# Attention probabilities transposed in pairs as 32-bit words, and two keys to a partition in the gathered V

## The chip, the core and the metric

The kernel runs on one core of a Trainium2 chip. The metric is the device time of one execution in microseconds (us), lower is better. A core has a matrix engine (TensorE, in the profile PE, with its weight loads as PEld), VectorE (DVE), ScalarE (ACT), GpSimd (POOL), and SyncE (SP), which here only issues DMA transfers. Operands lie in SBUF, 128 partitions wide; matrix results go to eight PSUM banks, each of 2 KB a partition, and have to be copied out by DVE or ACT. Sixteen DMA engines move data between HBM and SBUF.

## What is computed

Block-sparse attention over 4 batches x 8 heads x 768 positions x 64 channels, in blocks of 32 positions (24 blocks), followed by a dense two-layer network over all 3072 tokens:

```python
scores = scale * np.matmul(q, k.transpose(0, 1, 3, 2))
mask = np.abs(blk_i - blk_j) <= 1
mask = mask | (blk_i == 0) | (blk_j == 0) | (blk_i == n_blocks - 1) | (blk_j == n_blocks - 1)
for qb in range(n_blocks):
    for kb in sampled_blocks[qb]:                      # three drawn blocks
        mask[qb*32:(qb+1)*32, kb*32:(kb+1)*32] = True
attn = softmax(np.where(mask, scores, -1e9))
x = (attn @ v)                                          # tokens x 512
h = x @ w_in                                            # 512 -> 2048
out = (h * sigmoid(beta * h)) @ w_out                   # 2048 -> 512
```

A query block in the middle sees eight key blocks: three drawn ones, three of its window, and the two global ones (first and last). The first and last query blocks see all 24. Inputs and output are float32, `sampled_blocks` are 64-bit integers.

## The kernel before, in words

**Work and its order.** All of the program is a list of tasks, each with an engine (or a choice of engines), a duration that its author gave it, dependences and a priority. `Plan.run` places them in time like a small simulator, with rules for PSUM banks and a DMA ring, and the program is written out in that order; each engine then runs its instructions in it. The durations in the plan steer the order only. Tasks of the two-layer network have late priorities, so they fill PE where attention leaves it free.

**Middle blocks.** They are worked in pairs: 11 pairs a batch, 44 in all, task names with the pair number n. For a pair, POOL copies the drawn key blocks out of the transposed K into `KG` (L566, addresses from registers), POOL or DVE copy the window and, the first time, the global blocks (L261). PE adds a mask row by a matmul with ones (L658; it hides drawn blocks that repeat, and window blocks that repeat a global one) and multiplies queries with keys (L668). DVE takes maxima (L679), ACT the exponentials with sums (L687), DVE the reciprocals (L693), POOL or DVE scale the probabilities `PP` in fp16 (L699). PE transposes them, eight transposes of 128 x 128 for a pair (L711), DVE copies the bank to `PT` (L715), PE multiplies with `VG` in 32 matmuls of 64 x 32 (L727), and ACT or DVE put the result into `xT` (L259, L261).

**V.** `VG` holds the gathered V rows of a pair: 128 keys on the partitions, two halves of 512 channels and two query blocks in the free dimension. V of a batch is first written in fp16 to a table `VT` in HBM (L535, L539), a row of 512 channels being 1 KB, and SP gathers blocks from it (L627): the window (192 KB for both query blocks), the global blocks, and six drawn blocks of 32 KB. For the first four pairs the drawn rows don't come by DMA: PE picks them with one-hot matrices (`sel`, L388, made on DVE from block numbers that PE spreads over the partitions, L379 and L381), six matmuls of 512 columns for each query block (L638), which ACT or DVE copy into `VG` (L259, L261). Later pairs of a batch copy the global rows from an earlier `VG` (`vres`).

**Global blocks.** First and last query block are worked in 16 units (`gs` to `gav`): scores against all keys (L759), softmax (L773 to L791), six transposes with keys taken in steps of six (L799), DVE's copy to `PTG` (L801), 48 matmuls a batch with V (L813).

**The two-layer network.** `h` (L868), tanh on ACT (L874), the product on DVE (L879), `y` (L896), scaling and store (L265, L914 to L917). Its weights are loaded and cast by POOL's DMA queue (L461, L467), as are K, Q and V of batches 1 to 3 (L491).

**Start.** K, Q and V of batch 0 come through SP (L433), DVE casts them (L442), PE transposes (L508), ACT and DVE copy out. The 66 needed block numbers come by one DMA of single words (L291), from which POOL makes offsets (L307, L309) and DVE the mask (L313 to L337). One fp32 transpose exists, for beta (L402).

Of the kernel before, what the change touches and what calls it, by code (L numbers as in the profile page):

```python
# [10 lines left out]
FP32 = mybir.dt.float32  # L11
# [171 lines left out]
def kernel(  # L183
# [11 lines left out]
    nc = tc.nc  # L195
# [26 lines left out]
    SR, SG0, SN, SG1 = 0, 3, 4, 7  # L222

    identity = sb("identity", [P, P])
    ones = sb("ones", [P, P])
    maskr = sb("maskr", [P, NB - 2, 5])
    mrow = sb("mrow", [1, (NB - 2) * 5])
# [16 lines left out]
    PTG = sb("PTG", [P, J, 4, P])  # L244
# [26 lines left out]
    sbl = sb("sbl", [1, NB, 3], I32)  # L271
# [15 lines left out]
    def emit_sbl():  # L287
        src = sampled_blocks.tensor
        import dataclasses
        h = dataclasses.replace(src, shape=[NB, 6], dtype=I32)  # L290
        nc.scalar.dma_start(out=sbl, in_=bass.AP(tensor=h, offset=0, ap=[[0, 1], [6, NB], [2, 3]]))  # L291
    t_sbl = add("sbl", "ACT", 0.5, emit_sbl, prio=-200, dma=0.3, hw=1)
# [5 lines left out]
    sm5 = sb("sm5", [1, NB - 2, 5], FP32)  # L298
# [6 lines left out]
    def emit_idx():  # L305
        V = nc.gpsimd
        V.tensor_copy(out=sf, in_=sbl[:, 1:NB - 1, :])  # L307
# [5 lines left out]
    def emit_mask0():  # L313
        V = nc.vector
        V.memset(sm5, 0.0)
        V.memset(sm5[:, 0:1, 3:4], 1.0)
        V.memset(sm5[:, NB - 3:NB - 2, 4:5], 1.0)
# [12 lines left out]
    def emit_mask2():  # L330
# [4 lines left out]
        V.tensor_copy(out=sm5[:, :, 0:3], in_=sd)  # L335
        V.tensor_scalar(out=mrow, in0=sm5[:, :, :].rearrange("o a b -> o (a b)"),
                        scalar1=NEG / D, scalar2=None, op0=ALU.mult)  # L337
    t_mrow = None
    for part, f in enumerate((emit_mask0, emit_mask1, emit_mask2)):
        t_mrow = add(f"mask.{part}", "DVE", 0.95, f, deps=[t_idx, t_iota, t_ident, t_mrow], prio=-66.5)  # L340
    NM = (NB - 2) * 5
# [9 lines left out]
    SC = NSEL * 2 * 3 * BLK  # L351
    SH = SC // 2
    sel16 = sb("sel16", [P, SC])
    sel45 = sb("sel45", [P, 2, SC])
    sel = [xT[:, j // 2, N_TOK - (2 - j % 2) * SC:N_TOK - (1 - j % 2) * SC] for j in range(4)] + [
        sel45[:, i, :] for i in range(2)]
    srow = sb("srow", [1, NSEL * 2 * 3])
    mrow32 = sb("mrow32", [1, BLK])
    c32 = sb("c32", [1, P])
    pji = sb("pji", [P, J], I32)  # L360
    pj = sb("pj", [P, J], FP32)
    mi32 = sb("mi32", [1, BLK], I32)

    def emit_selc():
        V = nc.gpsimd
        V.iota(pji, pattern=[[1, J]], base=0, channel_multiplier=J, allow_small_or_imprecise_dtypes=True)
        V.iota(mi32, pattern=[[1, BLK]], base=0, channel_multiplier=0, allow_small_or_imprecise_dtypes=True)
        V.tensor_copy(out=pj, in_=pji)
        V.tensor_copy(out=mrow32, in_=mi32)
        V.memset(c32, float(BLK))  # L370
    t_selc = add("selc", "POOL", 1.2, emit_selc, prio=-98.5)
    t_srow = add("srow", "POOL", 0.15, lambda: nc.gpsimd.tensor_copy(
        out=srow, in_=sf[:, 0:2 * NSEL, :].rearrange("o a r -> o (a r)")), deps=[t_idx], prio=-98)
# [581 lines left out]
```

## Time and profile before

| | |
|---|---|
| median of 3 runs | 315.34 us (314.88 to 317.26) |
| the profiled execution | 316.81 us, of which the span from first to last instruction is 315.0 |
| busy: PE, DVE, ACT, POOL | 291.3, 232.1, 212.4, 185.4 us |
| L711, transposes of pairs | 352 matmuls, 28.4 us busy, 225 ns each |
| L799, transposes of global units | 96 matmuls, 8.2 us busy, 222 ns each |
| L727, probabilities times V | 1408 matmuls, 31.5 us busy |
| L638, picks | 48 matmuls, 15.9 us busy |
| L627, gathers of V | 306 DMAs of SP, most of 32 KB |
| queue q1 (SP's) | 27088 packets, 25.32 MB |

The time of one matmul in the profile includes its way through the array; matmuls overlap, so 225 ns is not what one more costs. That is read from the distance of their starts, or from how long a group of them lasts. The profile also gives, for every idle stretch of an engine, what ended it, and the chain of work that ended last. The granted clock is the share of full speed that the throttle let TensorE have.

### The profile page before, as it was taken

The numbers are of one execution on the slowest core, as the hardware profiler recorded it, in microseconds if no ns is written. First come the engines' busy times: TensorE is split into PE (matmuls) and PEld (weight loads), VectorE is DVE, ScalarE is ACT, GpSimd is POOL, SyncE is SP. The second block draws the span as 40 slices with busy tenths as digits, with TensorE's granted clock in tenths as the row PEclk, the third lists the DMA queues.
The fourth block names the chain that finished last, engine by engine and source line by source line (L and its number), as shares of the span: only waits on it lengthen the run. The fifth ranks groups of instructions, "written<-read, shape, count | busy, mean of one in ns | idle before, by whom it ended". The sixth has DMA issues, their size and how long they took to land.

```text
span 315.0 us, 12633 instructions
## 1 busy us (share of the span) xinstructions
PE 291.3 (92%) x4569; PEld 179.8 (57%) x4569; DVE 232.1 (74%) x536; ACT 212.4 (67%) x625; POOL 185.4 (59%) x534
## 2 busy tenths in 40 slices
PE   0889869998989899999999999999999999999994
PEld 0645558756946676556556565545655555554671
DVE  2972785988899999999985478999679845670160
ACT  1753757875876989778785579857679835671361
POOL 3389985988388797599687354648836842200000
PEclk9999956999999999999999999999999999999999
DMA  7969999699976886345899752234233341100201
GB/s 248 354 138 209 218 212 194 125 202 248 204 152 133 250 151 137 109 129 100 151 171 242 175 152 77 67 115 109 83 90 90 84 138 49 35 1 33 100 2 67
DMA packets 41546, 43.70 MB, mean 139 GB/s; under 512 B 6152, under 2 KB 37000, under 8 KB 41484
## 3 DMA queue, kind: packets, MB, share of 16 engines
q1 hardware_dynamic: 27088, 25.32, 27.8%
q0 software_dynamic: 10784, 11.27, 24.1%
q10 hardware_dynamic: 3612, 6.30, 5.5%
q8 instruction: 36, 0.59, 0.8%
q14 instruction: 26, 0.21, 0.2%
HBM read 44.70 MB, written 9.44 MB: 172 GB/s over the span
## 4 chain that ended last, share of the span: by engine, by line
PE 68%; DMA 7%; DVE 7%; issue 5%; POOL 4%; SPq 3%; POOLq 1%; ACT 1%; DVEq 0%; ACTq 0%
PE bank L868 23%; PE bank L896 22%; PE bank L727 7%; PE bank L711 6%; DMA RQ<-in_q_dram 6%; PE bank L668 2%; SPq L627 2%; PE bank L658 2%; POOL KG L566 2%; PE bank L508 2%; DMA VG<-VT 1%; PE bank L638 1%; DVE SG L773 1%; POOLq L561 1%; DVE ST L679 1%
## 5 line engine op out<-in xcount | busy, mean ns | idle before, releaser
L699 POOL TENSOR_SCALAR PP<-PP,ST 128x256 f16<-128x256 f16 x176 | 83.5, 490 | 35.7 <-DVE ST L693 31.1
L868 PE MATMUL bank<-xT,w_in_sb 128*128 128x256 f16 (+1 forms) x512 | 94.9, 332 | 1.9 <-DVE g L879 1.3
L687 ACT ACTIVATE PP<-bank,ST 128x256 f16<-128x256 f32 x176 | 81.6, 485 | 17.5 <-DVE ST L679 14.3
L896 PE MATMUL bank<-w_out_sb,g 128*128 128x512 f16 x384 | 91.3, 380 | 0.8 <-DVE g L879 0.8
L874 ACT ACTIVATE t<-bank,beta_sb 128x512 f16<-128x512 f32 (+1 forms) x128 | 70.0, 595 | 18.6 <-PE bank L868 15.5
L879 DVE SCALAR_TENSOR_TENSOR g<-t,bank 128x512 f16<-128x512 f16 (+1 forms) x128 | 66.4, 547 | 19.6 <-ACT t L874 19.2
L566 POOL COPY KG<-KT 128x64 f32 x264 | 53.9, 253 | 34.1 <-PE bank L668 26.7
L868 PEld LDWEIGHTS <-w_in_sb 128*128 128x128 f16 x512 | 54.2, 115 | 26.5 <-issue 4.8
L679 DVE TENSOR_REDUCE ST<-bank 128x2 f32<-128x512 f32 x88 | 57.3, 680 | 10.7 <-PE bank L668 10.6
L896 PEld LDWEIGHTS <-g 128*128 128x128 f16 x384 | 34.7, 98 | 39.2 <-issue 4.5
L715 DVE COPY PT<-bank 128x1024 f16<-128x1024 f16 x44 | 30.2, 685 | 14.1 <-PE bank L711 13.6
L687 ACT ACTIVATION_READ_ACCUMULATOR PP<-bank,ST 128x1 f32 x176 | 38.2, 217 | 0.0
L727 PEld LDWEIGHTS <-VG 128*64 128x64 f16 x1408 | 27.4, 115 | 17.3 <-issue 13.1
L727 PE MATMUL bank<-PT,VG 128*64 128x32 f16 x1408 | 31.5, 186 | 4.3 <-issue 2.1
L265 ACT ACTIVATE osb<-bank 128x512 f32<-128x512 f32 x24 | 14.4, 599 | 22.8 <-PE bank L896 22.7
L711 PE MATMUL bank<-identity,PP 128*128 128x128 f16 x352 | 28.4, 225 | 0.5 <-DVE PTG L801 0.3
L711 PEld LDWEIGHTS <-PP 128*128 128x128 f16 x352 | 23.0, 100 | 7.6 <-POOL PP L699 0.9
L780 ACT ACTIVATE PG<-bank,SG 128x384 f16<-128x384 f32 x32 | 18.3, 578 | 5.2 <-DVE ST L693 2.3
L668 PE MATMUL bank<-KG,QT 64*32 64x256 f16 x704 | 18.8, 278 | 0.9 <-POOL KG L566 0.8
L791 POOL TENSOR_SCALAR PG<-PG,SG 128x768 f16<-128x768 f16 x14 | 13.2, 946 | 9.4 <-ACT PG L780 3.8
L259 ACT CAST xT<-bank 128x256 f16<-128x256 f32 x25 | 9.5, 381 | 12.8 <-PE bank L727 11.0
L773 DVE TENSOR_REDUCE SG<-bank 128x1 f32<-128x384 f32 x32 | 16.1, 546 | 0.6 <-PE bank L759 0.5
(94 smaller groups left out, 261.7 us busy)
## 6 DMA issues: line engine op xcount, KB each, us to landing
VG<-VT SPq DMA_DIRECT2D x244, 32.0 KB, 2.8
VG<-VT SPq DMA_DIRECT2D x40, 192.0 KB, 3.8
out_dram<-osb ACTq DMA_DIRECT2D x20, 256.0 KB, 2.2
RV<-in_v_dram POOLq DMA_DIRECT2D x6, 384.0 KB, 5.8
RK<-in_k_dram POOLq DMA_DIRECT2D x6, 384.0 KB, 6.3
RQ<-in_q_dram POOLq DMA_DIRECT2D x6, 384.0 KB, 6.0
VT<-Vn SPq DMA_DIRECT2D x3, 768.0 KB, 6.0
w_in_sb<-in_moe_w_in_dram POOLq DMA_DIRECT2D x8, 256.0 KB, 8.0
```

Of the source, the lines that this page charges most:

```text
L566: nc.gpsimd.tensor_copy(out=kg32[:, g, :, (SR + r) * W:(SR + r + 1) * W], in_=kt32[:, :, bass.ds(vals[3 * g + r], W)])
L668: nc.tensor.matmul(bk[u][hp * BLK:(hp + 1) * BLK, g * 256:(g + 1) * 256], lhsT=QT[b % 2][u * D:(u + 1) * D, hp, (i0 + g) * BLK:(i0 + g + 1 ...
L679: mx[n, u] = add(f"mx{n}.{u}", "DVE", 0.6, lambda n=n, u=u, sb_=sb_: nc.vector.tensor_reduce(out=sb_[:, 0, 2 * u:2 * u + 2], in_=bank(("S" ...
L687: nc.scalar.activation(out=pb[:, u, g, :], in_=bank(("S", n, u))[:, g * 256:(g + 1) * 256], func=AF.Exp, bias=sb_[:, 0, 2 * u + g:2 * u + ...
L699: (nc.vector if eng == "DVE" else nc.gpsimd).tensor_scalar(out=pb[:, u, g, :], in0=pb[:, u, g, :], scalar1=sb_[:, 2, 2 * u + g:2 * u + g + ...
L711: nc.tensor.transpose(out=o[:, s * P:(s + 1) * P], in_=pb[:, u, g, c * P:(c + 1) * P], identity=identity)
L715: ptv[n] = add(f"ptv{n}", "DVE", 0.61, lambda n=n: nc.vector.tensor_copy(out=PT[n % NPT], in_=bank16(("T", n))), deps=[tp[n]] + ([av[n - N ...
L727: nc.tensor.matmul(o[us, (g * NHP + hp) * BLK:(g * NHP + hp + 1) * BLK], lhsT=vgb[:, g, c, (2 * hp + u) * D:(2 * hp + u + 1) * D], rhs=pt[ ...
L868: nc.tensor.matmul(o[:, 0:TW], lhsT=w_in_v[:, c, f // 4, f % 4, :], rhs=xT[:, c, c0:c0 + TW], start=(c == 0), stop=(c == NHP - 1))
L874: lambda G=G, f=f, TW=TW, tt=tt: nc.scalar.activation(out=tt[:, 0:TW], in_=bank(("H", G, f))[:, 0:TW], func=AF.Tanh, bias=0.0, scale=beta_ ...
L879: lambda G=G, f=f, TW=TW, tt=tt, gg=gg: nc.vector.scalar_tensor_tensor(out=gg[:, f, 0:TW], in0=tt[:, 0:TW], scalar=1.0, in1=bank(("H", G, ...
L896: nc.tensor.matmul(o[:, :], lhsT=gg[:, f, s * P:(s + 1) * P], rhs=w_out_sb[:, f, :], start=(f == 0), stop=(f == N_FFC - 1))
```

## The change

- **Transposes.** Two neighbouring fp16 probabilities are read as one 32-bit word. A pair takes four fp32 transposes instead of eight fp16 ones, a global unit three instead of six. A partition of `PT` and `PTG` then holds two neighbouring keys, even and odd in turn, so the matmuls with V read every second element.
- **V in step with it.** A partition of `VG` holds two neighbouring V rows (2 KB that lie together in `VT`), a block 16 partitions instead of 32. Each gather moves the same bytes as 16 rows of 2 KB.
- **Picks by parity.** The one-hot matrices choose row pairs, three of them instead of six. For one pair, two groups (even and odd rows) of three matmuls each yield both query blocks at once; four copies of 48 rows take them to `VG` instead of two of 96 rows.
- **Order of key blocks.** Global blocks lie together at the end (slots 6 and 7) instead of at 3 and 7; the mask has four columns a block instead of five, and the mask matmul of the first and last pair of a batch writes four key blocks instead of five.
- **Block numbers.** They come with their upper halves in one contiguous row.
- **A full fp32 identity** is made on DVE (before, a corner of 4 x 4); the one-hot matrices get tiles of their own instead of a corner of `xT`.
- The plan's durations for some of these tasks and for the first three key copies are new.

```diff
-    sbl = sb("sbl", [1, NB, 3], I32)
+    sbl = sb("sbl", [1, NB, 6], I32)
...
-        nc.scalar.dma_start(out=sbl, in_=bass.AP(tensor=h, offset=0, ap=[[0, 1], [6, NB], [2, 3]]))
+        nc.scalar.dma_start(out=sbl, in_=bass.AP(tensor=h, offset=0, ap=[[0, 1], [6, NB], [1, 6]]))
...
     t_id32 = add("id32", "DVE", 0.2, lambda: nc.vector.tensor_copy(
-        out=ident32, in_=identity[0:4, 0:4]), deps=[t_ident], prio=-64)
+        out=ident32, in_=identity), deps=[t_ident], prio=-64)
...
     t_sel = [add(f"sel16.{j}", "DVE", 0.27, lambda j=j: nc.vector.tensor_scalar(
         out=sel[j], in0=sel16, scalar1=pj[:, j:j + 1], scalar2=None, op0=ALU.is_equal),
-        deps=t_selw, prio=-66.2) for j in range(J)]
+        deps=[t_selw], prio=-66.2) for j in range(JP)]
...
-        kg[n] = add(f"kg{n}", "POOL", 1.15, emit_kg, deps=[t_idx] + kdeps, prio=pr)
+        kg[n] = add(f"kg{n}", "POOL", (1.5, 2.6, 1.35)[n] if n < 3 else 1.15, emit_kg, deps=[t_idx] + kdeps, prio=pr)
...
                 for r in range(3):
                     yield 0.1, lambda v, g=g, r=r: (
-                        vgb[r * BLK:(r + 1) * BLK, g, 0, :], vt[bass.ds(v[3 * g + r], BLK), :])
+                        vgb[(SR + r) * HB:(SR + r + 1) * HB, g, :, :],
+                        vt[bass.ds(v[3 * g + r], BLK), :].rearrange("(x e) m -> x e m", e=2))
...
-        for g in range(2 if n < NSEL else 0):
-            def emit_pick(n=n, g=g):
-                for j in range(J):
-                    c = (2 * n + g) * 3 * BLK
-                    nc.tensor.matmul(bank(("V", n, g))[0:3 * BLK, :], lhsT=sel[j][:, c:c + 3 * BLK],
-                                     rhs=Vn[0][:, j, :], start=(j == 0), stop=(j == J - 1))
+        for e in range(2 if n < NSEL else 0):
+            def emit_pick(n=n, e=e):
+                c = n * P
+                for j in range(JP):
+                    nc.tensor.matmul(bank(("V", n, e))[:, :], lhsT=sel[j][:, c:c + P],
+                                     rhs=Vn[0][:, 2 * j + e, :], start=(j == 0), stop=(j == JP - 1))
...
+            for g in range(2):
+                picked.append(add(f"pickv{n}.{e}.{g}", {"DVE": 0.61, "ACT": 0.58}, None,
+                                  lambda eng, n=n, e=e, g=g, vgb=vgb: copy_on(
+                                      eng, vgb[0:3 * HB, g, e, :],
+                                      bank(("V", n, e))[4 * HB * g:4 * HB * g + 3 * HB, :]),
+                                  deps=[tk], prio=pr - PK, closes=(("V", n, e),)))
...
-            ns = 5 if p in (0, NPAIR - 1) else 3
+            ns = 4 if p in (0, NPAIR - 1) else 3
...
         def emit_tp(n=n, pb=pb):
-            o = bank16(("T", n))
+            o = bank(("T", n))
             for g in range(2):
-                for c in range(2):
-                    for u in range(2):
-                        s = (g * 2 + c) * 2 + u
-                        nc.tensor.transpose(out=o[:, s * P:(s + 1) * P],
-                                            in_=pb[:, u, g, c * P:(c + 1) * P], identity=identity)
-        tp[n] = add(f"tp{n}", "PE", 0.45, emit_tp, deps=[nrm[n]], prio=pr - 0.5, lat=0.2,
+                for u in range(2):
+                    w = g * 2 + u
+                    nc.tensor.transpose(out=o[:, w * P:(w + 1) * P],
+                                        in_=pb[:, u, g, :].bitcast(FP32), identity=ident32)
+        tp[n] = add(f"tp{n}", "PE", 0.36, emit_tp, deps=[nrm[n], t_id32], prio=pr - 0.5, lat=0.2,
...
-                                rhs=pt[:, g, c, u, hp * BLK:(hp + 1) * BLK],
+                                rhs=pt[:, g, u, hp * BLK:(hp + 1) * BLK, c],
...
             def emit_gt(m=m, pg=pg):
-                o = bank16(("GT", m))
-                pj = pg[:, :].rearrange("x (p j) -> x j p", j=J)
-                for j in range(J):
-                    nc.tensor.transpose(out=o[:, j * P:(j + 1) * P], in_=pj[:, j, :], identity=identity)
+                o = bank(("GT", m))
+                pw = pg[:, :].bitcast(FP32).rearrange("x (p j) -> x j p", j=JP)
+                for j in range(JP):
+                    nc.tensor.transpose(out=o[:, j * P:(j + 1) * P], in_=pw[:, j, :], identity=ident32)
...
-                            rhs=PTG[:, j, u::2, hp * BLK:(hp + 1) * BLK],
+                            rhs=PTG[:, j // 2, u::2, :].rearrange("x w (m e) -> x w m e", e=2)[:, :, hp * BLK:(hp + 1) * BLK, j % 2],
```

## The prediction

> **What bounds the kernel now.** I read the page's chain by engine first, then the stage table (busy time of each engine in five stretches that I chose), then the chain and the timeline of the stretches that the diff touches, and last the single groups.
>
> ```profile
> PE 68%; DMA 7%; DVE 7%; issue 5%; POOL 4%; SPq 3%; POOLq 1%; ACT 1%; DVEq 0%; ACTq 0%
> 13.00:35.00 22.00, 19.94 (x200) 10.94 (x194) 13.41 (x33) 11.42 (x34) 20.07 (x57) 1.00 0.92 196
> 35.00:48.00 13.00, 8.93 (x250) 7.13 (x243) 9.86 (x24) 8.72 (x35) 11.37 (x28) 0.65 1.07 220
> 48.00:110.00 62.00, 58.47 (x1090) 42.45 (x1090) 54.79 (x141) 48.12 (x152) 46.38 (x123) 0.96 0.87 188
> 110.00:275.00 165.00, 163.04 (x2786) 94.94 (x2781) 133.82 (x286) 122.02 (x368) 104.80 (x312) 1.00 0.48 117
> ```
>
> The columns of the last four are the stretch, its length, busy us of PE, weight loads, DVE, ACT and POOL, the granted clock, the DMA engines' share and GB/s. From 110 to 275 us PE is busy 163 of 165: time taken from PE there comes off the end. From 13 to 48 us POOL (31.4 of 35) and the DMA engines (0.92, then 1.07) are full, and PE is not. So every edit is priced by where it falls: PE time counts in full from 48 us on, and before it only where the chain runs over PE.
>
> **The transposes (L711, L799).** Removed: 352 + 96 transposes of 128 two-byte columns; added: 176 + 48 of 128 four-byte words. Everything hangs on what one word transpose costs.
>
> ```profile
> 212.96 0.49 PEld L711 LDWEIGHTS <-PP 128*128 128x128 f16 x8
> 213.02 0.61 PE L711 MATMUL bank<-identity,PP 128*128 128x128 f16 x8
> 16.05 0.55 PEld L402 LDWEIGHTS bank<-t,osb 4*128 4x128 f32 x4 [0.17 <-issue]
> 16.05 0.64 PE L402 MATMUL bank<-t,osb 4*128 4x4 f32 x4
> 14.63 1.49 PE L508 MATMUL bank<-identity,RQ 128*64 128x128 f16 x24 [1.07 <-ACT QT L265]
> 123.10 0.79 PE bank L508 x24
> 42.95 1.02 PE bank L711 x8
> ```
>
> Now: eight in 0.61 us of which the last lasts 0.219, so (0.61 - 0.22)/7 = 0.056 us each, 0.45 us a pair; six of L799 0.336. The nearest row for a word is L402, the beta transposes: 128 words loaded, 4 columns streamed. Four loads of 0.208 (mean) lie in 0.55 us, so they start (0.55 - 0.21)/3 = 0.113 apart; its matmuls (0.64, mean 0.262) give 0.126. I take 0.12. PE ran at about half speed then: L508's 24 transposes take 1.49 us at 14.63 and 0.79 at 123.10 (the clock column shows 1.00 before 25 us only because nothing was recorded). At full speed 0.12 becomes 0.06. What 124 more columns add is not in the trace, so I bound it:
> - 0.06, if the next load runs beside the stream, as L711's loads do: 4 in 0.24, 0.21 saved a pair and 0.156 for each of the 16 global units, 44 x 0.21 + 16 x 0.156 = 11.7 us saved.
> - 0.113, if load and stream take turns: 0.06 + 124 columns at 0.43 ns (0.056/128). A pair costs 0.45, as now.
> - 0.267, if a word needs four streams. At half speed a two-byte transpose of 128 columns takes (1.02 - 0.31)/7 = 0.10, so a load of 128 words should too; the rest of L402's 0.12, some 0.015, is more than the 0.003 of four single columns, and would be four times four. At full speed 0.05 for the load and 4 x 0.054 for the streams.
>
> I take 0.10: L402's spacing is more than its load alone, which speaks for taking turns, with a little overlap. Saved: 44 x (0.45 - 0.40) + 16 x (0.336 - 0.30) = 2.8 us.
> The Trainium skill ("TensorE: Matmul & The Clock Gate", Terms, the row on the xbus) says that trn2's transpose mode is four times faster for FP32; by that rule the four-stream end falls away, and the sum with it. Against the change stands the same page's section on weight-path perf modes: fast weight load is not used with FP32 input, so a word load is slow and harder to hide; L402's load (0.208, against 0.098 of L711, though at the lower clock) agrees, and a sum by this rule loses the 2.8 us of the transposes.
>
> **AV and the global AV (L727, L813).** They now read every second element of PT and PTG. The chain has 48 matmuls of 64 columns (L813) in 0.76 us at 79.21 and 32 of 32 columns (L727) in 0.49 at 79.97: 16 ns and 15 ns. Twice the columns cost nothing, so the 64-column loads set the pace and a stream of half speed is still covered in AV. Without that cover, 13 ns on 32 columns: up to 16 pairs of matmuls x 13 ns x 44 = 9 us. I take 0.
> DVE's copies of PT and PTG move the same elements from the same banks: 0. The mask matmuls (L658) lose 64 of 320 columns in 8 pairs of 44: 0.2 us in all.
>
> **The head: picks, selection, block numbers.** Picks (L638) go from 48 to 24 of 512 columns.
>
> ```profile
> 29.79 1.29 PE bank L638 x6
> 31.50 1.43 PE bank L638 x6
> 33.38 1.29 PE bank L638 x6
> 36.60 1.38 issue
> 35.03 0.58 PEld L727 LDWEIGHTS <-VG 128*64 128x64 f16 x32 [0.21 <-DMA VG<-VT]
> DMA to landing us min/median/max: 4.0/7.1/12.4
> ```
>
> They are 4.0 us of the chain just ahead of the first AV; half is 2.0. But that AV starts 0.21 us after it could, on a VG transfer: without the picks the transfer is next, and 0.2 is all that comes unless it lands sooner. The last line is L627's (the VG gathers) from 14 to 50 us: up to 12.4 us to land. All VG rows now go as 2 KB runs instead of 1 KB. Prices from the queue table: q10's 3612 packets (6.30 MB, 5.5% of 16 engines' 315 us) take 77 ns for a mean of 1.7 KB; q1's 27088 (25.32 MB, 27.8%) take 52 ns for a mean of 0.93 KB. So 2 KB costs about 90 ns against 2 x 56, a fifth less. From 21 to 110 us 6.4 MB of VG are gathered: 3200 x 22 ns / 16 engines = 4.4 us less of queue. SP issues as many DMAs as before, 16 rows for 32. I take 1.5 us at the first AVs (between 0.2 and 3.4, the 2.0 of picks plus the 1.38 of the AV that sat at 36.60) and 1 us from the K, Q and V loads of batch 1 (11.1 us of the chain wait for RQ at 67 to 78; bounds 0 and 4.4).
> Block numbers come as one run of 576 bytes instead of 72 single words; POOL waits for them till 6.06 us. Eight small DVE mask operations then lie at 6.3 to 8.1 and five at 9.0 to 10.1, ahead of the second pair of K casts at 10.00. Six selection compares of 0.40 (2.4 us) become three of about 0.3. That brings K's cast about 0.9 us forward, and POOL's key copies at 13.24, with which the chain goes on, wait for K (ACT's KT): 0.9 us. If K's own transfer is late, 0.
> Added: evictions of picks go from 8 to 16, of the same columns (0.58 on ACT, 0.69 on DVE): 4.9 us. ACT has 10.6 and DVE 8.6 us idle from 13 to 35, which hides them; without that cover the last, 0.6 us, is late for the first AV. The full word identity on DVE (128x128, about 0.25 by the cast of maskr) lies before 6 us. POOL gains one small memset (0.2) in its idle time up to 13.24.
>
> **Sum.** 2.8 + 0.2 + 1.5 + 1.0 + 0.9 = 6.4 us off. The profiled execution took 316.81 (span 315.0 and 1.8 around it), 1.5 above the median of the runs, 315.34. So about 310.4 for an execution like the profiled one, and 309.0 for the median.
>
> **Rivals.**
> 1. A word is dear because four bytes stream at half speed: twice 0.054 for the stream, once or twice that for the load, taking turns: 0.16 to 0.213 a transpose. For it: L402 streams only four columns, so no row shows a word stream at two-byte speed. Against it: its four columns add no more than 0.02 to the load. Place: PE, L711 and L799, in the stretch where PE is full; price 224 x 0.16 - 25.2 = 10.6 to 22.5 us more, less the other 3.6: 322 to 334. It decides from 224 x cost = 25.2 + 3.6, that is 0.129 us a word transpose.
> 2. Four streams, 0.267: 34.6 us more, less 3.6: 346. For it speaks L402's spacing, as worked out; against it that the spacing may hold a fixed gap instead. The Trainium skill ("FP8 and Floating Point Precision", TensorE Precision Notes) counts four passes for a true FP32 product; L402 cannot tell whether that holds for a transpose, and the rule of the four times faster mode speaks against it.
> 3. Loads run beside the streams, 0.06: 11.7 + 3.6 off, 300. Then POOL (105 of 165 us) and DVE (134) are still below PE, so most of it arrives: 300 to 305.
> 4. The head gives nothing and the word transpose costs as now. A new order from the planner, the longer wait for VG, or PE at half clock for longer (0.65 from 35 to 48 now, after idle PE; fewer picks leave it idler) takes the 3.6 back: 313 to 318. Here belongs that the gathers still move 1 KB at a time: then q1's packets don't fall.
>
> **Chances.** Forecast (305 to 312) 0.38; rival 3 0.17; rival 4 0.17; rival 1 0.17; rival 2 0.11. A measurement of this kernel tells about 1% (3.2 us) from no change. Faster: forecast and rival 3, 0.55; within 1%: 0.17; slower: rivals 1 and 2, 0.28. The range reaches from rival 3's lower end to rival 1's upper: 300 to 334, leaving out rival 2 and a little below. The likeliest case alone: 305 to 312.
>
> **What would show it.** L711's matmuls: four with starts 0.10 apart and about 0.4 us a pair in the chain; 0.06 or 0.16 and more are the rivals. L727's 32 still in 0.5 to 0.6 us. The first AV at about 32.5 instead of 35.0, the first L868 at about 45 instead of 47.8. q1 at some 19,500 packets with the same MB. The first KG copy of POOL at about 12.3. The prediction is wrong if the word transposes start more than 0.129 us apart, or if the first L868 comes no sooner.

## The result: slower by 7.6%, and the profile after

| | before | after |
|---|---|---|
| median (lowest to highest) of 4 executions | 316.29 us (314.88 to 317.26) | 343.68 us (338.29 to 347.0) |
| ratio, 95% interval | | 1.076 [1.062, 1.089] |
| the profiled execution, its span | 316.81, 315.0 us | 345.37, 343.3 us |

Ratios here and below leave out executions that were disturbed, medians don't; the profiles of the changed kernel, of its two versions with nothing repaired but the stores (words and fp16), and of the changed work in the order of before come from executions that were left out, so what is read there of SP's waits is given from another profile too. Lines have moved: L627 is now L631 (gathers of V), L711 L718 (pairs' transposes), L727 L734 (probabilities times V), L799 L806, L868 L875, L896 L903.

The chain by engine, the stage table over the same stretches (stretch, length, busy us of PE, weight loads, DVE, ACT and POOL, granted clock, DMA share, GB/s), SP's queue and two groups of the changed kernel:

```profile
PE 48%; DMA 20%; DVE 14%; SPq 6%; ACT 4%; issue 4%; POOL 2%; POOLq 1%; DVEq 0%; ACTq 0%
13.00:35.00 22.00, 12.75 (x164) 5.94 (x158) 17.03 (x35) 10.84 (x33) 19.73 (x60) 0.84 0.88 186
35.00:48.00 13.00, 6.45 (x165) 4.76 (x166) 4.55 (x14) 5.84 (x25) 5.71 (x19) 0.50 0.92 174
48.00:110.00 62.00, 57.64 (x990) 42.76 (x989) 53.84 (x135) 45.41 (x144) 42.38 (x107) 0.94 0.84 170
110.00:275.00 165.00, 146.37 (x2322) 85.76 (x2321) 124.23 (x264) 110.72 (x340) 100.19 (x303) 0.95 0.47 113
q1 hardware_dynamic: 18576, 25.32, 25.2%
L734 PE MATMUL bank<-PT,VG 128*64 128x32 f16 x1408 | 33.2, 189 | 22.7 <-DMA VG<-VT 15.6
L718 PE MATMUL bank<-ident,PP 128*128 128x128 f32 x176 | 30.3, 296 | 12.7 <-POOL KG L565 7.8
```

PE's share of the chain has fallen from 68 to 48%, and DMA's has risen from 7 to 20. From 110 to 275 us PE now idles 18.6 of 165 us; it idled 2.0 before. PE's work has not grown: it is busy 293.2 us, before 291.3. The products with V (L734) wait 15.6 us for gathered rows, but 10.5 of that lies between 30 and 60 us and only 1.3 between 110 and 275. There most of the idle time is two stretches, 5.9 us up to 158.5 and 7.8 us up to 238.1, and both come through DVE. When DVE's next instruction copies global rows that SP has gathered (`vres`), and these are late, everything behind it is late too: the first time pair 21's PT, the second time the softmax of the global units, for which POOL waits 7.7 us. DVE's waits for such rows (us in total, times, longest):

```profile
DVE VG L264 <- DMA VG<-VT: 14.2, 2, 8.0
```

Half the clock (0.50) is granted from 158 to 164 and from 233 to 243 us. Of all twenty profiles, DVE waits like this (4.3 to 15.6 us) in the eight where SP's gathers wait over 40 us for stores, and in none of the other twelve. So the loss is waiting, and the waiting is for V.

What SP, which issues those gathers, waited for (line, what ended the wait, us in total, times, longest). Before:

```profile
SPq L627 <- PE bank L727: 16.2, 8, 6.6
SPq L627 <- DMA VT<-Vn: 4.8, 2, 2.5
SPq L627 <- DMA out_dram<-osb: 0.9, 1, 0.9
```

After:

```profile
SPq L631 <- DMA out_dram<-osb: 56.0, 12, 10.0
SPq L631 <- DMA VT<-Vn: 14.7, 1, 14.7
SPq L631 <- PE bank L734: 1.9, 4, 1.0
```

Before, SP ran so far ahead that it waited for a VG tile to come free (L727, 16.2 us). Now it waits 56 us for **output stores**, 4.7 us each time on average, and it has nothing to do with them: ACT issues them. The link is in the waits of the program. The DMAs of SP and ACT report their end on eight semaphores in rotation, and a DMA may use one only when the DMA eight places earlier in the program's list has landed. The Trainium skill says why it must wait ("DMA: Bandwidth & Descriptors", Why a DMA increments its semaphore by 16 and not by 1): with two DMAs in flight on one semaphore the count can reach the first one's mark before that one has fully landed, so each wants one of its own. The same page (Anatomy of one DMA) has such a wait happen on the issuing sequencer; the trace agrees, as SP's own queue stands still.

One such case in the changed kernel, first SP's and ACT's timelines (start, length, line, operation), then the chain (start, length, what):

```profile
130.77 8.23 SPq L631 DMA_DIRECT2D VG<-VT  x4
135.98 0.34 ACTq L923 DMA_DIRECT2D out_dram<-osb  x1
```

```profile
151.01 0.72 SPq L594
151.85 0.33 SPq L631
152.23 4.67 DMA VG<-VT
157.00 0.70 DVE VG L264
157.72 0.70 DVE PT L722
158.47 1.04 PE bank L734 x32
```

SP issues four gathers in 8.23 us, because one of them waits 6.4 us for the store that ACT can issue only at 135.98, when `y` and its scaling are done; the store lands at 138.17 and the gather, on the same semaphore, goes at 138.19. After that SP needs 0.5 us for a DMA, seven for a pair, and doesn't catch up: the global rows of the third batch's first pair are issued at 151.85, land at 156.9, DVE copies them at 157.0 and only then pair 21's PT, and PE's product with V follows at 158.47. PE is busy 17.81 of the 25 us from 150 to 175. In the second stretch the chain itself runs over a store, SP and the copy:

```profile
225.65 2.00 DMA out_dram<-osb
227.67 0.33 SPq L631
...
232.51 2.10 DMA VG<-VT
234.70 1.30 DVE VG L264 x2
```

The second loss is at the head. Timelines of SP and POOL in the changed kernel:

```profile
14.55 2.06 SPq L534 DMA_DIRECT2D VT<-Vn  x2
31.34 2.70 SPq L631 DMA_DIRECT2D VG<-VT  x6
```

```profile
15.26 1.98 POOL L460 DMA_DIRECT2D w_in_sb<-in_moe_w_in_dram  x3 [0.30 <-POOL w_in_sb L446]
```

POOL's key copies start at 10.42 instead of 13.24, and so the weights' loads, which stand behind them on POOL, at 15.26 instead of 19.66. V's table is stored only 1.9 us sooner, at 14.55 instead of 16.48. So the first weight load now starts before the table's second half (15.26 against 16.08) and two more right behind it, by 16.72, and the second half lands at 31.3; the first gather waits 14.7 us for it. Before, it landed at 21.5, with the weights' loads behind it. The first product with V starts at 38.6 instead of 35.0, the first with `w_in` at 53.4 instead of 47.8, and PE idles half of the time from 35 to 48 us, with half the clock granted (0.50). This second loss is not in every execution of this order: see the fp16 version below. The Trainium skill ("TensorE: Matmul & The Clock Gate", Part 1: The HAM clock gate) gives half clock after an idle window of about 3.4 us; the trace agrees as far as it goes: PE is busy 1.42 us from 24 to 28, and 0.50 is granted from 28 us on.

### The profile page after: what moved, and what is told of

Its sections match the earlier page's. It is cut to its first block, busy times and chain, and to the rows that moved or that the text cites. A ratio compares the mean times of both kernels' runs of the same rounds, so it can differ in the third digit from the quotient of the medians.

```text
span 343.3 us, 12204 instructions
## 1 busy us (share of the span) xinstructions
PE 293.2 (85%) x4319; PEld 179.6 (52%) x4319; DVE 237.2 (69%) x536; ACT 211.9 (62%) x627; POOL 183.7 (54%) x537
## 3 DMA queue, kind: packets, MB, share of 16 engines
q1 hardware_dynamic: 18576, 25.32, 25.2%
## 4 chain that ended last, share of the span: by engine, by line
PE 48%; DMA 20%; DVE 14%; SPq 6%; ACT 4%; issue 4%; POOL 2%; POOLq 1%; DVEq 0%; ACTq 0%
PE bank L875 17%; PE bank L903 16%; DMA VG<-VT 12%; PE bank L734 5%; SPq L631 5%; DMA VT<-Vn 4%; PE bank L718 4%; ACT PP L694 2%; DVE ST L686 2%; DMA out_dram<-osb 2%; DVE g L886 2%; PE bank L507 2%; DVE PT L722 1%; PE bank L675 1%; DMA g<-in_k_dram 1%
## 5 line engine op out<-in xcount | busy, mean ns | idle before, releaser
L706 POOL TENSOR_SCALAR PP<-PP,ST 128x256 f16<-128x256 f16 x172 | 81.3, 488 | 62.7 <-DVE ST L700 59.9
L875 PE MATMUL bank<-xT,w_in_sb 128*128 128x256 f16 (+1 forms) x512 | 96.3, 335 | 0.3 <-DVE g L886 0.3
L903 PE MATMUL bank<-w_out_sb,g 128*128 128x512 f16 x384 | 92.6, 383 | 0.6 <-ACT PP L694 0.4
L875 PEld LDWEIGHTS <-w_in_sb 128*128 128x128 f16 x512 | 55.6, 115 | 26.6 <-issue 5.3
L903 PEld LDWEIGHTS <-g 128*128 128x128 f16 x384 | 35.5, 98 | 39.9 <-issue 5.1
L734 PE MATMUL bank<-PT,VG 128*64 128x32 f16 x1408 | 33.2, 189 | 22.7 <-DMA VG<-VT 15.6
L734 PEld LDWEIGHTS <-VG 128*64 128x64 f16 x1408 | 29.2, 119 | 38.1 <-issue 26.5
L718 PE MATMUL bank<-ident,PP 128*128 128x128 f32 x176 | 30.3, 296 | 12.7 <-POOL KG L565 7.8
L694 ACT ACTIVATION_READ_ACCUMULATOR PP<-bank,ST 128x1 f32 x176 | 37.4, 212 | 0.0
L718 PEld LDWEIGHTS bank<-ident,PP 128*128 128x128 f32 x176 | 21.6, 148 | 20.6 <-POOL KG L565 8.4
L262 ACT CAST xT<-bank 128x256 f16<-128x256 f32 x30 | 11.2, 374 | 32.5 <-PE bank L734 19.2
L787 ACT ACTIVATE PG<-bank,SG 128x384 f16<-128x384 f32 x32 | 18.3, 592 | 14.7 <-DVE SG L782 11.7
L780 DVE TENSOR_REDUCE SG<-bank 128x1 f32<-128x384 f32 x32 | 16.1, 545 | 2.0 <-PE bank L766 2.0
```

The source lines that it names most:

```text
L694: nc.scalar.activation(out=pb[:, u, g, :], in_=bank(("S", n, u))[:, g * 256:(g + 1) * 256], func=AF.Exp, bias=sb_[:, 0, 2 * u + g:2 * u + ...
L706: (nc.vector if eng == "DVE" else nc.gpsimd).tensor_scalar(out=pb[:, u, g, :], in0=pb[:, u, g, :], scalar1=sb_[:, 2, 2 * u + g:2 * u + g + ...
L718: nc.tensor.transpose(out=o[:, w * P:(w + 1) * P], in_=pb[:, u, g, :].bitcast(FP32), identity=ident32)
L734: nc.tensor.matmul(o[us, (g * NHP + hp) * BLK:(g * NHP + hp + 1) * BLK], lhsT=vgb[:, g, c, (2 * hp + u) * D:(2 * hp + u + 1) * D], rhs=pt[ ...
L875: nc.tensor.matmul(o[:, 0:TW], lhsT=w_in_v[:, c, f // 4, f % 4, :], rhs=xT[:, c, c0:c0 + TW], start=(c == 0), stop=(c == NHP - 1))
L903: nc.tensor.matmul(o[:, :], lhsT=gg[:, f, s * P:(s + 1) * P], rhs=w_out_sb[:, f, :], start=(f == 0), stop=(f == N_FFC - 1))
```

## The experiments

### Is it the transposes, the planner's durations or the weights' loads?

**Transposes back to fp16**, order and layout as in the changed kernel:

```diff
-                    nc.tensor.transpose(out=o[:, w * P:(w + 1) * P],
-                                        in_=pb[:, u, g, :].bitcast(FP32), identity=ident32)
+                        nc.tensor.transpose(out=o[:, s * P:(s + 1) * P],
+                                            in_=pb[:, u, g, c::2], identity=identity)
```

> The changed kernel with its own order of work, V gathered two keys to a partition as there, but the probabilities of the pairs turned by eight two-byte transposes (every second key as weights) instead of four of 32-bit words, and read back to back. Only the pairs' transposes differ; the planner's prices, and so the order, are the changed kernel's. If the loss comes from SP's gathers (waits for the V table and for output stores), the time stays with the changed kernel: 338 to 347 us. If the word transposes or the stepped reads of PT cost it, it falls towards the kernel before: below 325.

Measured: 347.36 us, 1.103 [1.093, 1.112] of the kernel before. SP waits 57.9 us for stores in 13 waits, and from 110 to 275 us PE idles 18.7. In this execution the weights' loads came at 17.67 and V's table was ready at 19.3, so the first product with V started at 31.9, and still the end was as late. Neither the words nor the late table is the main cause.

**The changed work with the old durations in the plan:**

```diff
-        tp[n] = add(f"tp{n}", "PE", 0.36, emit_tp, ...
+        tp[n] = add(f"tp{n}", "PE", 0.45, emit_tp, ...
```

(and the other six durations that the change touched, back to what they were)

> The changed kernel's work with the planner's prices of before for the transposes (0.45, 0.44), the first key copies (1.15), the block numbers and the V gathers. The work is the same, the order of issue is not. If the loss is an order that makes SP wait for stores, an order from other prices moves the time by 3% or more, most likely down, to 312 to 330 us. If it is the cost of the work itself, 338 to 347 stays.

**The work of before with the new durations:** the same edit the other way round.

> The work of the kernel before with the planner's prices of the change (transposes 0.36 and 0.30, key copies 1.5, 2.6, 1.35, block numbers 0.1, gathers a fifth cheaper). If the new prices alone bring the bad order, 325 to 345 us; if the order comes from the changed task list or the work itself is dear, 313 to 319.

Measured: 333.49 us, 1.057 [1.049, 1.065], and 324.0 us, 1.027 [1.019, 1.035], each between the two ranges that were expected. The order that the new durations give costs 8 us with unchanged work, so it has a part. With the changed work SP waits 49.7 us for stores under the old durations too; with the old work 1.5 under the new ones. So most of the loss doesn't come from the durations.

**Weights loaded after V's table**, by making the load that starts them read the table:

```diff
-    tch = touch(w_in_sb[0:1, 0, 0:1], v_stage[0:1, 0, 0:1], v0ld[0], -58)
+    scr = sb("scr", [1, 2])
+    tch = add("touch", "POOL", 0.6, lambda: nc.gpsimd.dma_start(
+        out=scr[0:1, 0:1], in_=VT[0][0:1, D_MODEL - 1:D_MODEL]), deps=[v0ld[0]], prio=-58)
...
+    tch.deps += vtab[0]
```

> The changed kernel, but the loads of the network's weights start only once the V table of batch 0 has landed (POOL waits for it through a one-element read of the table). In the changed kernel the table's second half takes until 31.3 us while weights are loaded beside it. If that contention holds the first AV back (38.6 us, against 35.0 before), the table lands by about 21 us, the first AV comes at 27 to 32, and the time falls by 3 to 9 us to 332 to 340; the stalls later in the run stay. If the table is late for another reason, neither moves.

Measured: 344.19 us, 1.094 [1.083, 1.104], so the 3 to 9 us expected did not come. The head does what was asked: SP's wait for the table falls from 14.7 to 2.6 us and the first product with V starts at 30.0 instead of 38.6. Nothing of this is left at the end, and SP's waits for stores have grown to 64.1 us:

```profile
SPq L633 <- DMA out_dram<-osb: 64.1, 13, 11.2
SPq L633 <- DMA VT<-Vn: 2.6, 1, 2.6
```

### Stores out of the rotation

If POOL issues the stores, they are counted elsewhere, and no gather waits for one.

```diff
-                    nc.scalar.dma_start(out=out[base + row:base + row + P, :], in_=ob)
+                    nc.gpsimd.dma_start(out=out[base + row:base + row + P, :], in_=ob)
...
-            out_dma.append(add(f"od{G}.{s}", "ACT", 0.4, emit_od, ..., dma=0.7, hw=1))
+            out_dma.append(add(f"od{G}.{s}", "POOL", 0.6, emit_od, ..., dma=0.7))
```

> The changed kernel, but POOL issues the output stores instead of ACT. In the traces a gather of SP waits until the DMA eight places earlier in the program, among those of SP and ACT, has landed; an output store eight places back costs SP 10 us each time (56 us over 12 waits in the changed kernel). Theory A, these waits carry most of the loss: SP's waits on out_dram fall from 56 us to below 5, and the time from 342 to 318 to 330. Theory B, the waits are only where lateness that has another cause comes to light (late V table, SP's own 0.5 us for a DMA, a poorer order on PE): another wait takes their place and the time stays at 337 to 347.

> Control: the kernel before, with its output stores issued by POOL. SP waits only 0.9 us for stores there, so by theory A nothing is to be won: 314 to 319. If POOL's added work (about 50 DMAs at its own pace) is what counts, it is slower, 318 to 325, and the same then has to be taken off the reading of the changed kernel with stores by POOL. If it is 305 to 311, stores on ACT cost something in both kernels, and theory A does not explain the difference between them.

> The changed kernel with stores by POOL, and the pairs' transposes as eight fp16 ones that step over the keys, PT read back to back; plan and order as in the changed kernel with stores by POOL. If word transposes are neutral, as four of them took 0.55 to 0.59 us in the chain and eight fp16 ones 0.55 to 0.61, it is within 1% of that kernel. If words save what the prediction said, it is about 3 us slower; if the words' cost at half clock (0.214 us from start to start, against 0.12) counts, it is 3 to 8 us faster.

The last run joins this edit with the two before (weights after the table, old durations):

> All three suspected costs off: the changed kernel with stores by POOL, weights loaded only after the V table has landed, and the planner's durations of the kernel before. Theory A: 308 to 320, at or below the kernel before, as the first product with V starts near 30 us instead of 35 and nothing on SP waits for stores. Theory B (the layout or the transposes cost on PE as such): it stays above 325.

| run | us | ratio to before |
|---|---|---|
| changed kernel, stores by POOL | 327.29 | 1.031 [1.021, 1.041] |
| kernel before, stores by POOL | 319.95 | 1.010 [1.002, 1.019] |
| the first, with fp16 transposes | 326.24 | 1.030 [1.022, 1.038] |
| the first, with the table first and old durations | 318.21 | 1.005 [1.001, 1.009] |

SP's waits in the changed kernel with stores by POOL:

```profile
SPq L631 <- DMA VT<-Vn: 15.2, 2, 14.4
SPq L631 <- PE bank L734: 14.6, 14, 2.0
SPq L631 <- DMA VG<-VT: 7.2, 7, 1.7
```

No gather waits for a store any more, SP again waits for tiles to come free (14.6 us; 15.0 in the last version), and the ratio falls from 1.076 to 1.031, some 14 us. The kernel before wins nothing and loses 3.3: its last product with V starts at 273.6 us as before, but its span is 318.7 instead of 315.0. The last store is issued only 0.4 us later (312.19 against 311.79) and has landed by 314.4; what lasts is POOL's closing drain, to 317.8. That much of the edit's cost is in the changed kernel's 327.29 as well. Words against fp16: 327.29 and 326.24, no difference that can be told. Moving the stores also lets the planner write the order anew; the crossed runs below repeat the comparison.

### What is left: head, order, end

The last five stores back to ACT, after SP's last gather has gone, for the version with all three repairs; the same two edits in the kernel before; and each repair of the head or order alone with all stores by POOL:

```diff
+            q_ = nc.gpsimd if nout < 19 else nc.scalar
...
-                    nc.scalar.dma_start(out=out[base + row:base + row + P, :], in_=ob)
+                    q_.dma_start(out=out[base + row:base + row + P, :], in_=ob)
```

> The changed kernel with its three repairs (stores by POOL, weights' loads after the V table, planner's durations of the kernel before), but the last five stores go back to ACT: when all stores are POOL's, the last one ends the program later (last product with V at 273.6 us in both kernels before, spans 315.0 and 318.7). Expected 313 to 316, some 3.5 us below the 318.2 of the version with all stores on POOL; if the end of the program is set by something else, 317 to 319.

> The kernel before with the same two repairs that can be made in it: stores by POOL but for the last five, and weights' loads after the V table. Theory A, words and two keys to a partition bring next to nothing on PE, and head and order are all: it is as fast as the repaired changed kernel within 1%, 312 to 317. If the change itself brings its 3 to 5 us once nothing on SP is in its way, the repaired changed kernel is faster than this by 1 to 1.5%, and this comes out at 316 to 319.

> The changed kernel with stores by POOL and weights' loads after the V table, but the planner's new durations. Against 327.3 with the stores alone and 318.2 with all three repairs: if the order that the new durations give costs most of what is left, it stays at 324 to 328; if the late V table does, it comes to 318 to 321.

> The other half: stores by POOL and the planner's old durations, with the weights' loads where the changed kernel has them, ahead of the V table's second half. If the order costs most of what is left: 318 to 321. If the late V table does: 324 to 328. If each has a part, both this and its counterpart come out between 320 and 325.

| run | us | ratio to before |
|---|---|---|
| three repairs, last stores by ACT | 314.37 | 0.996 [0.991, 1.001] |
| kernel before with stores and table edited alike | 327.95 | 1.033 [1.028, 1.039] |
| stores by POOL and table first | 318.89 | 1.008 [1.005, 1.012] |
| stores by POOL and old durations | 319.05 | 1.007 [1.003, 1.012] |

By the ratios either repair takes off 7 us, both together 8 (318.21): they are not separate costs. With the old durations POOL starts two weight loads early instead of three, and the table is ready at 24.3 instead of 31.1, so both may act through the table; that was not separated. The end is worth 3 to 4 us, as expected. The fully repaired kernel is level with the kernel before, not faster.

The second row was a miss on both sides of its expectation: 11 us slower than before, with no gather waiting for a store. Its chain shows a new order in the head:

```profile
41.63 2.52 ACT PP L689 x11
...
44.92 1.42 DVE PP L701 x4
...
48.83 2.72 PE bank L713 x24
```

Three pairs' transposes stand together at 48.83 behind exponentials and scalings, the fourth product with V at 51.5 instead of 44.9, and the first with `w_in` at 54.0 instead of 47.8. So one more dependence, with the new order that the planner makes of it, can cost more than the work in question, and no comparison in which the order is written anew tells a few us of work.

### Work and order crossed

So the order was fixed. Each task of one kernel was written out in the place, on the engine and in the PSUM bank that the other kernel's plan gives it:

```diff
-    order = plan.run()
+    by_name = {t.name: t for t in plan.tasks}
+    order = [by_name[nm] for nm, _ in ORDER_OF_THE_OTHER]    # engines and banks from there too
```

> The changed kernel's work, written out in the order of the kernel before: every task on the engine, in the place and in the PSUM bank that the kernel before gives it (the two halves of the row-number matmul and copy at the place of the second; a pick's two copies at the place of its one copy; three one-hot matrices at the place of the first three). Theory O, the order is the whole loss and the work itself is neutral to slightly better: 311 to 318, SP's waits on out_dram below 3 us. Theory W, the new work (word transposes, 2 KB rows of V, four copies for a pair's picks) costs time where the order is the same: 325 or more.

> The crossing: the work of the kernel before in the changed kernel's order, engines and banks (the row-number halves one after the other in one bank, two one-hot matrices at the place of each of the three, a pick's one copy at the place of the first of its two). Theory O: 335 to 347, with SP waiting 40 us or more for output stores. Theory W: 314 to 322.

> The changed kernel in the order of the kernel before, but the pairs' transposes as eight fp16 ones that step over the keys. The price of the word transposes of the pairs, without stalls of SP between: 2.0 to 3.0 us more than the first of these three if words save what the prediction said (44 pairs, 0.49 against 0.55 us); within 1 us if four words take as long as eight fp16 transposes (0.55 to 0.59 against 0.55 to 0.61 us); 2 us or more less if words at half clock are the dearer ones.

Measured: 336.42 us, 1.063 [1.055, 1.072]; 323.91, 1.026 [1.019, 1.033]; 335.89, 1.056 [1.042, 1.070]. The order of before doesn't help the first, so theory O misses; it has the time that theory W gave (325 or more), but not for W's reason: what costs is again SP's wait, not PE's work. The second is 2 us above W's range. SP in the first run (44.4 us in 12 waits in the third) and in the second:

```profile
SPq L799 <- DMA out_dram<-osb: 53.7, 12, 10.3
SPq L799 <- PE bank L902: 3.3, 2, 3.1
```

```profile
SPq L795 <- PE bank L895: 18.2, 11, 5.8
SPq L795 <- DMA out_dram<-osb: 6.2, 1, 6.2
```

The stalls follow the work, not the planner's order; the 2.6% of the second run are the order's part, like the 2.7% of the new durations. The built programs show how that can be. In each, the DMAs of SP and ACT stand in one list, 347 of them, and that list is what the rotation counts. The first ten stores stand at these places, counted from 0:

```
kernel before                        66  77 106 114 144 156 159 204 212 227
changed kernel                       57  68  87  93 128 134 136 190 195 203
changed work, order of before        56  63  87  94 124 131 132 188 199 206
work of before, changed order        69  75 106 107 144 152 153 201 213 224
changed work, order of before, but
  V gathered as 32 rows of 1 KB      66  76 106 114 144 155 158 203 211 226
```

The order within each engine is the planner's, but how the engines' instructions are laid into one list is not: it changes with the form of the gathers. With 16 rows of 2 KB every gather stands some 15 places later against PE and ACT. When the product of pair 10 stands in the list, 79 gathers stand before it in the kernel before, 63 in the changed work in the same order. The last row was only built, not run: with the gathers' form alone put back, the places are those of before within one. So a gather that was two pairs early now stands behind a store that comes shortly before its rows are needed.

### Moving the stores, and the price of the work alone

Each store was moved later in ACT's stream, in the crossed kernel and in the changed kernel's own order:

```diff
     order = plan.run()
+    for t in out_dma:                        # 14 us later by the plan, but ahead of the next use of its tile
+        ...
+        order.insert(j, order.pop(i))
```

> Crossing work and order fell both ways: the changed work in the order of the kernel before took 336.4 us with SP waiting 53.7 us for stores, the other crossing 323.9. In the built programs the list that all engines' DMAs are counted in is not the planner's: of the 347 DMAs of SP and ACT, the stores stand at places 66, 77, 106, 114, 144, 156, 159 in the kernel before, at 57, 68, 87, 93, 128, 134, 136 in the changed one and at 56, 63, 87, 94, 124, 131, 132 with the changed work in the order of before. So the changed work moves the stores 8 to 25 places ahead of the gathers, and gathers then wait for stores that come later in time. Here: the changed work in the order of before, each store moved later in ACT's stream (some 14 us by the plan), which puts them at 70, 83, 104, 110, 145, 170, 172. Theory S, the places are the whole loss: 313 to 320 and SP's waits for stores below 10 us. If the new work costs of itself: 325 or more, with the time in PE's waits for PP or PT.

> The changed kernel in its own order, each store moved later in ACT's stream by some 14 us of the plan: places 75, 83, 104, 108, 148, 153, 155 instead of 57, 68, 87, 93, 128, 134, 136. Theory S: the 56 us of SP's waits for stores go, as they did when POOL issued the stores (327.3), but without the 3.6 us that POOL's stores cost at the end: 321 to 327. What is left over before is then the late V table and the order. If it stays at 336 to 347, moving stores to POOL helped for another reason.

And the changed work in the order of the kernel before with stores by POOL, so that both kinds of work stand in one order and no gather waits for a store in either:

> The changed work in the order, engines and banks of the kernel before with stores by POOL (319.95 us): no store shares a semaphore with a gather in either, and the order is the same, so the difference is the work itself (words, 2 KB rows, picks, mask, block numbers, weights' loads). The prediction's sum by steps would give 313 to 316; neutral work 317 to 322; work that costs, 325 or more.

Measured: 335.71 us, 1.061 [1.055, 1.067]; 335.78, 1.058 [1.052, 1.065]; 320.53, 1.005 [1.001, 1.010].

The first two miss: SP still waits 43.7 and 52.0 us for stores. Theory S, that the places are what counts, is wrong as I put it. A store that is moved in ACT's stream comes later in time as well, and the gather eight places behind it with it; that reading is argued and not shown by a run of its own, since gathers were not moved earlier. How far SP is ahead can be counted in the traces. When pair 15's product with V starts, it has issued so many of 306 gathers:

| | gathers issued | us |
|---|---|---|
| kernel before, stores by POOL | 116 | 319.95 |
| kernel before | 116 | 316.29 |
| changed work, order of before, stores by POOL | 119 | 320.53 |
| changed kernel | 109 | 343.68 |
| changed work, order of before | 106 | 336.42 |
| the same, stores later | 100 | 335.71 |

The three slow ones are one to two pairs of seven gathers behind.

The third run is the clean comparison. Against 319.95 (1.010) the same order with the changed work takes 320.53 us (1.005): **the work itself is neutral**, to within about 1%. It also shows once more what the stores cost: with the changed work in an order of the kernel before, 1.063 with stores by ACT and 1.005 with stores by POOL. Its chain:

```profile
164.49 9.07 DMA RQ<-in_q_dram
173.56 0.04 issue
173.60 0.86 PE bank L675 x24
...
266.19 0.44 PE bank L886 x4
271.68 0.44 PE bank L886 x4
```

The head gains here what was forecast: the first product with V starts at 30.8 us instead of 34.6, the first with `w_in` at 43.5 instead of 46.8. But at pair 15 the lead is 1.0 us, and at 173.6 PE waits for Q of batch 3, whose load POOL issued at 164.5 and which took 9.07 us. From pair 27 on both kernels run 0.2 us apart to the end.

## Why the prediction was wrong

The forecast was 309.0 us and faster; it became 343.7. The steps for PE came out near what they said, but for the transposes. What failed is the step that priced the gathers by their queue alone, with the words "SP issues as many DMAs as before, 16 rows for 32". The number is right (306), but when SP can issue them was taken as given. In its place the runs showed SP's waits for stores: 0.9 us before, 56.0 after, and some 14 us of the time (1.076 to 1.031) once they are gone. Of the two signs by which the prediction called itself wrong, the first product with `w_in` coming no sooner came true (53.4 against 47.8 us); words more than 0.129 us apart did not.

- **What bounds the kernel.** Right for before. That PE was full from 110 to 275 us rested on SP being 2 pairs ahead; its waits (16.2 us for free tiles, 0.9 for stores) show that cover and the link that can end it, and the prediction makes no use of them.
- **Transposes.** 0.10 us a word was taken; the words start 0.109 us apart at full clock (and 0.214 at half), next to the bound of 0.113 for load and stream in turns. The spacing fits turns, but also a load that is hidden behind a stream of half speed; the traces don't tell which. A word's load lasts 0.140 us at full clock, a two-byte one 0.098. A pair takes 0.44 us to the next matmul, eight fp16 ones 0.45. So the term was 2.8 us and is about 0.4: 44 x 0.01, and for the global units 16 x (0.336 - 3 x 0.109) = 0.1. Rivals 1, 2 and 3 are out, as 0.129 was not reached and 0.06 neither. Of three couples of kernels that differ in the pairs' transposes alone (words first), two are within about 1 us, 327.29 and 326.24, 336.42 and 335.89; in the third, 343.68 and 347.36, words are 1% faster or more, with SP stalled in both.
- **AV.** Right: the 32 matmuls take 0.61 us or a little more in the chain, as in most of its rows before, and in the one order they cost the same busy time (31.3 us before, 31.1 after).
- **2 KB rows.** q1's packets fell to 18,576 with the same MB (19,500 was said). Their time barely fell: 27.8% of 16 x 315.0 us is 1401 us, 25.2% of 16 x 343.3 is 1384. 17 us over 8512 packets saved is 2 ns, not 22, for each two that became one; a 2 KB packet takes about 110 ns, not 90. In the one order it is 26.8% of 318.7 against 25.7% of 318.8, or 6.5 ns. The 1 us for batch 1's loads had no ground.
- **The head.** 1.5 and 0.9 us were forecast together with 32.5 for the first product with V. In the same order without stalls it is 3.8 us sooner, so more than said; in the changed kernel it is 3.6 us later, because V's table lands at 31.3 among the weights' loads. The block numbers did more than I said: POOL's first key copy starts at 10.42, from 13.24, where I took 12.3. What I left out is what stands behind those copies on POOL, the weights' loads: they moved forward by 4.4 us and the table by 1.9, into each other.
- **A lead at the head is not a gain at the end.** I added 3.4 us of head to the sum as if nothing later had its own clock. In the one order the lead fell to 1.0 us by pair 15 and went into one late load.
- **Rival 4** named a new order, a longer wait for VG and PE at half clock, which is what happened. It was priced at the 3.6 us that it could take back. Measured: the new durations alone 8 us (324.0), the stores' waits some 14, the table or the order 7 more. A mechanism that stops PE is not limited by what the other steps win.

Settled is that waits of gathers for stores carry most of the loss, that either repair of head or order takes most of the rest, and that words, layout and picks together cost nothing of themselves to within about 1%. Not tried is a copy of the global rows that can't hold up DVE, by another engine or by a gather for each pair. Open is why the list depends on the form of the gathers, and whether gathers moved earlier in it would do what the stores moved later did not.

## What to carry to other kernels

Before pricing an engine's work, look at what the DMA issuer waits for: if it waits for free buffers it has cover, and if it waits for a transfer that has nothing to do with it, the completion semaphores are shared, and a change of form can turn that into a stall of PE. Keep stores that depend on late compute out of the rotation that early loads use; another issuer did it here, at some 3 us if the last stores go with it; the last five back on ACT won that again. A copy that waits for a transfer should not stand in the stream of an engine whose later work PE needs. Where a planner writes the order anew, compare two kinds of work in one fixed order: new durations alone moved this kernel by 8 us.

## What the runs showed of the hardware that I had not expected

- Transposing 128 x 128 words of four bytes takes 0.109 us from start to start at full clock and 0.214 at half; the two-byte one takes 0.056. Two for one, so nothing is won by words.
- By the queue's shares of time a packet of 2 KB takes about as long as two of 1 KB (105 to 110 ns against 112), though 32 KB gathers land sooner (2.4 us against 2.8 in the median).
- A store of 384 KB was issued at 16.1 us in each of three executions. With weight loads of POOL's queue starting at 15.26, 16.17 and 16.72 it landed at 31.3; with 14.80, 16.23 and 17.83, at 24.3; with the first at 17.67, at 19.3.
- SP needs about 0.5 us for each gather, some 4.2 us for a pair with its register load. PE's products with V come 5.6 us apart on average in the kernel before (35.0 to 273.6 us, 44 pairs), so by estimate SP gains 1.4 us a pair, and a stall of 6 us takes four or five pairs to make good.
- When POOL issues the last stores, its closing drain ends at 317.8 us, though the last of them has landed by 314.4. With ACT as the issuer, and the last store issued 0.4 us sooner, the whole span ends at 315.0.
